# First feed-forward chunk in float32 from the arriving tiles, early loads into idle tiles of the second sweep, and early splits placed by hand

## The chip, the core and the metric

The kernel runs on one core of one Trainium2 chip. The metric is device time in microseconds (us), lower is better. The engines are TensorE (PE in the profile; its weight loads are PEld), VectorE (DVE), ScalarE (ACT), GpSimd (POOL) and SyncE (SP), which here only issues transfers. Each engine works through its own queue in the order in which it was written.

## The reference

One input x of 2048 tokens by 512 goes through two branches, mixed per token by a gate. Everything is float32.

```python
x = A_x                                              # 1 x 2048 x 512
g = sigmoid((x * gate_w).sum(-1, keepdims=True))
a = A(x)    # linear attention, 32 heads of 16
b = relu(x @ w1 + b1)**2 @ w2 + b2                   # 512 -> 1792 -> 512
out = g * a + (1 - g) * b

# A: q, k, v = x @ wqkv; pq = q @ w_phi per head, pk likewise
# phi = concat(softmax(p), softmax(-p));  kv = phi_k^T v;  z = sum of phi_k over tokens
# o = (phi_q kv) / (phi_q z + 1e-6);  A = o @ wo
```

## The kernel before

**Products in three parts.** A float32 operand is split into a high half in the format fp32r and a low half, the rest (`split`, L58: a copy on ACT, then a subtraction on DVE). A product is three matmuls that add into one PSUM bank: high by high, high by low, low by high (`mm3`, L66 to L70). A plain float32 matmul on the unsplit tiles would give the same product; the kernel uses those only for the folds (`fold`, L138: w_phi multiplied into the q or k weights), for the key-value sums (`kv_chunk`, L217) and for the numerators (`numer`, L263).

**Two sweeps.** x is worked in four blocks of 512 tokens, the hidden layer in 14 chunks of 128 columns. Sweep 0 takes, for each block, chunks 0 to 6, and beside them the k and v projections and the key-value sums; its half of the feed-forward result goes to DRAM (`part`). Sweep 1 takes chunks 7 to 13 and beside them the q projections, the division and the output projection. One step of `work_list` (L510) is one chunk of one block: an *up* product (12 matmuls of 512 columns into bank `u`), then on ACT a relu, a square and a copy, on DVE the low half (`hidden`, L301), and a *down* product (12 matmuls into four banks `d`). Up runs two steps ahead of down (`LAG`, L25). "Up 2" below is the up product of chunk 2 of the first block, and "down 0" the down product of chunk 0; "k 0", "v 0" (the first k, the first v) are projections of the first 128 tokens, also 12 matmuls each. K and v share one PSUM bank once the folds are done (L329), so each waits until the one before has been read: k by the four DVE steps in `exps` (L199 to L202), v by an ACT copy (L407).

**The order.** `at(slot, f)` (L464) hangs pieces of work on slots, two for each step, and the tile framework turns the written order and its priorities into one fixed queue for each engine; `tc.issue_after(i)` puts an instruction behind `i` on the same engine. Tiles with one tag share the buffers of that tag, so a load waits for the last reader of the buffer that it takes over. Most weights and x come through four `stage` tiles (L36, `load` L76), the fold's weights, the gate's rows of x (`gate_load` L168) and the results through six `row` tiles (L81). Tiles that only sweep 1 uses (`phiT`, `tb`, `oh`, `ol`) stand empty in sweep 0.

**The start.** `warm_up` (L350) issues 11 matmuls on zeros. `start` (L361) loads x's four parts and the first w1 chunk (a quarter and the rest on ACT's queue), splits each part as it arrives (a part of the weight on POOL, L381), and runs the first chunk's twelve products with six more zero matmuls between them (L385 to L393). W1 chunks 1 and 2 and w2 chunk 0 are split right behind (L521, L526). The other weights of sweep 0, Wv and the next block's x are each loaded and split in one step at their slots (L469 to L481), so the splits follow the arrivals.

Of the kernel before, what the change touches and what calls it, by code (L numbers as in the profile page):

```python
# [1 line left out]

# [6 lines left out]
F32 = mybir.dt.float32  # L9
# [7 lines left out]
P = 128  # L17
S, D, H, DH, F = 2048, 512, 32, 16, 1792
NK = D // P
SB = 512  # L20
# [11 lines left out]
def tile_gated_mix(ctx: ExitStack, tc: tile.TileContext, xT, xn, wqT, wkT, wphi, wv, wo, w1, b1, w2, b2, gw, out):  # L32
# [12 lines left out]
    ps_a = pool("ps_a", 1, space=PSUM)  # L45
    ps_b = pool("ps_b", 1, space=PSUM)
    banks = [ps_a, ps_b]
    taken = [0]

    def bank(name):  # L50
# [7 lines left out]
    def split(src, hi, lo, ehi, elo):  # L58
        if ehi is nc.scalar:
            i = nc.scalar.activation(hi, src, AF.Copy)  # L60
        else:
            i = ehi.tensor_copy(hi, src)
        elo.tensor_tensor(lo, src, hi.bitcast(F32), ALU.subtract)  # L63
        return i

    def mm3(o, a, b, sa, sb, first, last):  # L66
# [21 lines left out]
    def load_ffn(nm, src, fc):  # L88

        if (nm, fc) in (("w1", 1), ("w1", 2), ("w2", 0)):  # L90
            t = row()
            nc.sync.dma_start(t, src)
        else:
            t = load(src)
        hi, lo = ffn_tiles(nm, fc)
        split(t, hi, lo, nc.scalar, nc.vector)
        return hi, lo

    def load_x(b):
        xs = []  # L100
        for k in range(NK):
            t = load(xT[b, :, k, :])
            hi = xpool.tile([P, SB], F32R, tag="xh", name=f"xh{b}_{k}")
            lo = xpool.tile([P, SB], F32R, tag="xl", name=f"xl{b}_{k}")
            split(t, hi, lo, nc.scalar, nc.vector)
            xs.append((hi, lo))
        return xs

    st, up_w, down_w = {}, {}, {}
    hold = pool("hold", 2)  # L110
    ident = const.tile([P, P], F32, name="ident")
    make_identity(nc, ident)
# [25 lines left out]
    def fold(loaded, nm, k):  # L138
# [8 lines left out]
            split(ps, hi, lo, nc.scalar, nc.vector)  # L147
        return hi, lo

    def load_w(src, nm):  # L150
        res = []
        for k in range(NK):
            if nm == "o":

                t = stage.tile([P, 512], F32, tag="in", name="in")
                for q in range(4):
                    s = 64 * (4 * (k % 2) + q) + 32 * (k // 2)
                    nc.sync.dma_start(t[32 * q:32 * q + 32, :], src[s:s + 32, :])
            else:
                t = load(src[k * P:(k + 1) * P, :])  # L160
            hi = wpool.tile([P, 512], F32R, tag=f"wbh{k}", name=f"w{nm}h{k}")
            lo = wpool.tile([P, 512], F32R, tag=f"wbl{k}", name=f"w{nm}l{k}")
            split(t, hi, lo, nc.scalar, nc.vector)
            res.append((hi, lo))
        return res


    def gate_load(n):  # L168
        st["xn", n] = row()
        nc.sync.dma_start(st["xn", n], xn[n])  # L170

    def gate_chunk(n):
        t = st["xn", n]
        lg = small.tile([P, 1], F32, tag="lg", name="lg")
        nc.vector.scalar_tensor_tensor(t, t, 1.0, gwb, op0=ALU.mult, op1=ALU.mult, accum_out=lg)
        e = small.tile([P, 1], F32, tag="ge", name="ge")
        nc.scalar.activation(e, lg, AF.Exp, scale=-1.0)
        nc.vector.tensor_scalar(e, e, 1.0, None, ALU.add)
# [84 lines left out]
    def numer(pt):  # L263
# [15 lines left out]
                mm(*x)  # L279
        o = []  # L280
        for r in range(2):
            oh = work.tile([P, 512], F32R, tag=f"oh{r}", name="oh", bufs=1)
            ol = work.tile([P, 512], F32R, tag=f"ol{r}", name="ol", bufs=1)
# [31 lines left out]

    def down(t, c, dps):
        sw, b, i = work_list[t]
        mm3(dps[c], hid[t], down_w[sw * NFH + i], slice(c * P, (c + 1) * P), ALL, i == 0, i == NFH - 1)

    def do_wT(wT):  # L320
        st["wT"] = load_fold(wT)
# [9 lines left out]
    def do_w(src, nm):  # L331
        st["wb"] = load_w(src, nm)

    def do_w1_first(fc):
        with tc.issue_after(st["act0"].ins):
            do_w1(fc)

    def do_w1(fc):
        up_w[fc] = load_ffn("w1", w1[fc], fc)

    def do_w2(fc):
        down_w[fc] = load_ffn("w2", w2[fc * P:(fc + 1) * P, :], fc)

    def do_ffn(fc):
        do_w1(fc)
        do_w2(fc)

    def warm_up():  # L350
        z = st["zeros"] = work.tile([P, 512], mybir.dt.bfloat16, tag="r", name="zeros")
        nc.vector.memset(z, 0.0)
        st["warm"] = ps_a.tile([P, 512], F32, tag="s", name="warm")
        idle(11)

    def idle(n):
        for _ in range(n):
            st["up"] = nc.tensor.matmul(st["warm"], st["zeros"][:, :P], st["zeros"], start=True, stop=True)


    def start():  # L361
        t = row()
        hi, lo = up_w[0] = ffn_tiles("w1", 0)
        xs = st["x", 0] = []
        ps = ps_u.tile([P, SB], F32, tag="u", name="u")
        for k in range(NK):
            s = slice(0, P) if k == 0 else slice(P, 512)
            u = load(xT[0, :, k, :])
            if k == 0:
                for piece in (s, slice(P, 512)):  # L370
                    nc.scalar.dma_start(t[:, piece], w1[0][:, piece])
            xs.append((xpool.tile([P, SB], F32R, tag="xh", name=f"xh0_{k}"),
                       xpool.tile([P, SB], F32R, tag="xl", name=f"xl0_{k}")))
            if k == 0:
                split(t[:, s], hi[:, s], lo[:, s], nc.vector, nc.vector)
            nc.scalar.activation(xs[k][0], u, AF.Copy)
            low = nc.vector.tensor_tensor(xs[k][1], u, xs[k][0].bitcast(F32), ALU.subtract)
            if k == 0:
                rest_w = slice(P, 512)
                with tc.issue_after(low.ins):  # L380
                    split(t[:, rest_w], hi[:, rest_w], lo[:, rest_w], nc.vector, nc.gpsimd)  # L381
            (xh, xl), kk = xs[k], slice(k * P, (k + 1) * P)
            with tc.issue_after(st["up"].ins):
                st["up"] = nc.tensor.matmul(ps, hi[:, kk], xh, start=k == 0, stop=False)
            if k < 2:  # L385
                with tc.issue_after(st["up"].ins):
                    idle(2)
            with tc.issue_after(st["up"].ins):
                nc.tensor.matmul(ps, hi[:, kk], xl, start=False, stop=False)
                st["up"] = nc.tensor.matmul(ps, lo[:, kk], xh, start=False, stop=k == NK - 1)  # L390
            if k < 1:
                with tc.issue_after(st["up"].ins):
                    idle(2)  # L393
        st["u0"] = ps

    def do_x(b):
        with tc.issue_after(st["act"].ins):
            st["x", b] = load_x(b % NB)

    def do_k(b, c):  # L400
        e3, r = exps(project(c, st["x", b], st["wa"], "k"))
# [62 lines left out]
    def at(slot, f, *a):  # L464
        steps.setdefault(int(slot), []).append(lambda: f(*a))

    at(6, lambda: nc.sync.dma_start(gwb, gw.partition_broadcast(P)))
# [50 lines left out]

    warm_up()
    start()  # L520
    for fc in range(1, LAG + 1):  # L521
        do_w1(fc)
    hid[0] = hidden(0, st["u0"])
    st["act0"] = st["act"]
    with tc.issue_after(st["act0"].ins):
        for fc in range(LAG + 1):  # L526
            do_w2(fc)
    for t in range(1, LAG):
        do_up(t)
    dps = None  # L530
    for t, (sw, b, i) in enumerate(work_list):
        for f in steps.get(2 * t, ()):
            f()
        do_up(t + LAG)
        for f in steps.get(2 * t + 1, ()):
            f()
        if i == 0:
            dps = [ps_d.tile([P, 512], F32, tag="d", name=f"d{c}") for c in range(NC)]

        now = () if t == last - 1 else (t - 1, t) if t == last else (t,)  # L540
        for c in range(NC):
            for u in now:
                down(u, c, dps)
        if i < NFH - 1:
            continue
        for c in range(NC):
# [63 lines left out]
```

## Time and profile before

| | us |
|---|---|
| median of 3 runs | 533.31 (532.88 to 533.75) |
| the profiled execution, whole | 533.63 |
| its span, first to last instruction | 531.8 |

Of the 531.8 us, TensorE was busy 521.5, VectorE 355.9, ScalarE 234.7 and GpSimd 76.8. In a row of the timeline stand the start, the busy time, the engine, the line, the operation, the tiles (out<-in) with their shapes, how many instructions were merged into the row, and in brackets the idle time before it with what ended it. A float32 matmul leaves two rows. Matmuls overlap in the pipeline, and their ends are modelled: their rate is read from start to start. A row of the busy time by stage has the stage, its length, the busy time and count of each engine, the granted TensorE clock, the busy share of the DMA engines and their GB/s.

### The profile page before, as it was taken

To read this page: it belongs to the slowest core of one execution; us is meant where nothing else is said; L and a number is where in the kernel's file an instruction comes from. 1 tells how busy PE (TensorE), PEld (TensorE's weight loads), DVE (VectorE), ACT (ScalarE), POOL (GpSimd) and SP (SyncE) were. 2 spreads that over 40 slices of the span, in tenths; PEclk is the share of its full clock that TensorE was granted. 3 is DMA by queue.
4 is the path that set the end of the run, shared out by engine and by line. 5 is a ranking of instruction groups with operands and counts; after the bars stand their busy time and mean duration, and the time that the engine had idled before them with its cause. 6 is when DMAs were issued, how large, how long until landed. Compare 5 with 4: busy or idle time off the path is not lost.

```text
span 531.8 us, 8944 instructions
## 1 busy us (share of the span) xinstructions
PE 521.5 (98%) x3475; PEld 417.5 (79%) x3475; DVE 355.9 (67%) x608; ACT 234.7 (44%) x404; POOL 76.8 (14%) x60
## 2 busy tenths in 40 slices
PE   8998999999999999999999999999999999999997
PEld 3886888888888887887878878787887878787775
DVE  4688536743465434567579998998878887779423
ACT  3874333622435224254654564353435353535230
POOL 2001111111110011011103121202111111112000
PEclk9999999999999999999999999999999999999999
DMA  7974004200042000415346113134102311023102
GB/s 236 297 240 138 2 0 160 76 6 1 1 159 70 10 1 21 160 41 160 88 139 222 35 41 122 53 118 137 40 22 79 119 51 30 22 70 100 49 1 79
DMA packets 30834, 45.16 MB, mean 85 GB/s; under 512 B 5704, under 2 KB 12360, under 8 KB 30792
## 3 DMA queue, kind: packets, MB, share of 16 engines
q1 hardware_dynamic: 30328, 44.20, 27.0%
q8 instruction: 27, 0.44, 0.3%
q10 hardware_dynamic: 432, 0.39, 0.2%
q14 instruction: 15, 0.12, 0.1%
q0 software_dynamic: 32, 0.01, 0.0%
HBM read 29.89 MB, written 8.39 MB: 72 GB/s over the span
## 4 chain that ended last, share of the span: by engine, by line
PE 72%; DVE 10%; DMA 6%; SPq 5%; ACT 3%; POOL 2%; issue 2%; DVEq 0%; ACTq 0%; POOLq 0%
PE u L68 7%; PE d L69 7%; PE d L70 7%; PE d L68 7%; PE u L70 7%; PE u L69 7%; SPq L257 4%; PE v L68 3%; PE k L68 3%; PE v L69 3%; PE v L70 3%; PE k L70 3%; PE k L69 3%; PE kvps L221 2%; DMA in<-in_xT 2%; PE att L68 2%
## 5 line engine op out<-in xcount | busy, mean ns | idle before, releaser
L303 ACT ACTIVATE r<-u,b1c 128x512 f32<-128x512 f32 x56 | 38.5, 687 | 151.3 <-PE u L70 148.0
L68 PE MATMUL d<-w2h,hh 128*128 128x512 f32 x224 | 87.5, 391 | 0.0
L69 PE MATMUL d<-w2l,hh 128*128 128x512 f32 x224 | 87.3, 390 | 0.0
L70 PE MATMUL d<-w2h,hl 128*128 128x512 f32 x224 | 87.1, 389 | 0.0
L68 PE MATMUL u<-xh,w1h 128*128 128x512 f32 x220 | 86.8, 395 | 0.1
L70 PE MATMUL u<-xh,w1l 128*128 128x512 f32 x220 | 85.7, 390 | 0.5 <-DVE w1l L63 0.5
L69 PE MATMUL u<-xl,w1h 128*128 128x512 f32 x220 | 85.8, 390 | 0.0
L63 DVE TENSOR_TENSOR hl<-r,hh 128x512 fp32r<-128x512 f32 x56 | 43.0, 769 | 54.8 <-ACT hh L60 54.7
L231 POOL TENSOR_TENSOR ez<-e,z 128x512 f32<-128x512 f32 x32 | 41.4, 1317 | 188.3 <-ACT e L204 188.3
L213 POOL TENSOR_TENSOR e<-e,r 128x1024 f32<-128x1024 f32 x16 | 32.3, 2017 | 205.0 <-DVE r L209 158.3
L207 DVE TENSOR_REDUCE sm<-e 128x64 f32<-128x1024 f32 x32 | 39.0, 1218 | 28.5 <-ACT e L204 28.4
L68 PEld LDWEIGHTS u<-xh,w1h 128*128 128x128 f32 x220 | 41.3, 188 | 12.0 <-issue 1.6
L70 PEld LDWEIGHTS d<-w2h,hl 128*128 128x128 f32 x224 | 42.0, 188 | 8.7
L68 PEld LDWEIGHTS d<-w2h,hh 128*128 128x128 f32 x224 | 42.0, 188 | 8.7
L69 PEld LDWEIGHTS d<-w2l,hh 128*128 128x128 f32 x224 | 42.1, 188 | 8.6
L70 PEld LDWEIGHTS u<-xh,w1l 128*128 128x128 f32 x220 | 41.3, 188 | 9.5 <-DVE w1l L63 0.9
L69 PEld LDWEIGHTS u<-xl,w1h 128*128 128x128 f32 x220 | 41.3, 188 | 8.2
L204 ACT ACTIVATE e<-e 128x1024 f32<-128x1024 f32 x32 | 33.8, 1055 | 23.7 <-DVE e L202 23.5
L255 ACT ACTIVATE phiT<-tb 32x256 f32<-32x256 f32 x64 | 26.5, 413 | 35.1 <-DVE tb L249 34.4
L60 ACT ACTIVATE hh<-r 128x512 fp32r<-128x512 f32 x56 | 35.2, 628 | 1.3
L304 ACT ACTIVATE r<-r 128x512 f32<-128x512 f32 x56 | 35.1, 627 | 1.0
L199 DVE TENSOR_REDUCE mx<-k 128x32 f32<-128x512 f32 x16 | 11.0, 688 | 26.3 <-PE k L70 26.3
(106 smaller groups left out, 888.5 us busy)
## 6 DMA issues: line engine op xcount, KB each, us to landing
in<-in_xT SPq DMA_DIRECT2D x32, 256.0 KB, 3.9
in<-in_w SPq DMA_DIRECT2D x24, 256.0 KB, 3.2
phiT<-tb SPq DMA_DIRECT2D x192, 32.0 KB, 1.8
row<-in_xn SPq DMA_DIRECT2D x16, 256.0 KB, 3.2
part<-row SPq DMA_DIRECT2D x16, 256.0 KB, 2.0
row<-part SPq DMA_DIRECT2D x16, 256.0 KB, 3.5
out<-row SPq DMA_DIRECT2D x15, 256.0 KB, 2.2
row<-in_wkT SPq DMA_DIRECT2D x4, 256.0 KB, 6.0
```

The costliest lines, as they stand in the source:

```text
L60: i = nc.scalar.activation(hi, src, AF.Copy)
L63: elo.tensor_tensor(lo, src, hi.bitcast(F32), ALU.subtract)
L68: nc.tensor.matmul(o, ah[:, sa], bh[:, sb], start=first, stop=False)
L69: nc.tensor.matmul(o, ah[:, sa], bl[:, sb], start=False, stop=False)
L70: return nc.tensor.matmul(o, al[:, sa], bh[:, sb], start=False, stop=last)
L204: nc.scalar.activation(ef, ef, AF.Exp)
L207: nc.vector.tensor_reduce(sm, e3, AX.X, ALU.add)
L213: eng.tensor_tensor(e3, e3, w.unsqueeze(2).to_broadcast([P, 2 * H, DH]), ALU.mult)
L231: nc.gpsimd.tensor_tensor(ez[:, hs, :], e3[:, hs, :], zbc[half], ALU.mult)
L255: nc.scalar.activation(dst, src, AF.Copy)
L303: nc.scalar.activation(r, ps, AF.Relu, bias=b1c[:, fc:fc + 1])
L304: nc.scalar.activation(r, r, AF.Square)
```

## The change

- The first chunk of the first block is four plain float32 matmuls on the tiles as they arrive. The low and high halves of x are still made, for the chunks after it; those of the first w1 chunk are made later, as the second block needs them. There are 8 zero matmuls ahead and none between.
- Loading (`fetch`) and splitting (`ready`) are separate. The first loads are issued one after the other at the start: x into a `phiT` tile, w1 chunks 0 to 2 and w2 chunk 0 into `tb` tiles, then w1 3, w2 1, the fold's weights, w1 4, w2 2, then Wv into the `phiT` tile again. Later blocks' x goes through `tb` tiles, the gate's rows through `oh` and `ol` tiles (now two of each tag in place of one each of four).
- Splits are hung on slots of their own and, with `issue_after`, behind the copy of the newest hidden tile on ACT (`st["act"]`) and the gate's product behind the newest subtraction on DVE (`st["low"]`).
- Up 1 follows the float32 chunk, down follows up and up follows down, by `issue_after`, in the first steps.

The queue of PE after the change has the same order as before from down 0 on, but for a few neighbours swapped. On DVE and ACT the order between down 0 and the end of sweep 0 is another: the halves of later weights, of Wv and of the next x, and the gate's products, stand further behind.

```diff
+    def ready_later(nm, fc):
+        with tc.issue_after(st["act"].ins):
+            ready(nm, fc)
...
     def gate_load(n):
-        st["xn", n] = row()
-        nc.sync.dma_start(st["xn", n], xn[n])
+        t = st["xn", n] = work.tile([P, D], F32, tag="ol" if n % 2 else "oh", name="xn", bufs=2)
+        nc.sync.dma_start(t, xn[n])
...
+        with tc.issue_after(st["low"].ins):
+            nc.vector.scalar_tensor_tensor(t, t, 1.0, gwb, op0=ALU.mult, op1=ALU.mult, accum_out=lg)
...
     def start():
-        t = row()
-        hi, lo = up_w[0] = ffn_tiles("w1", 0)
...
+        t = work.tile([P, 2, 4, NG, 32], F32, tag="phiT", name="xin", bufs=1).rearrange("p u r g s -> p (u r g s)")
+        w = [work.tile([P, 2 * D], F32, tag="tb", name="win", bufs=2) for _ in range(2)]
+        raw["w1", 0] = w[0][:, :D]
+        xs = [t[:, k * D:(k + 1) * D] for k in range(NK)]
+        for k in range(NK):
+            nc.sync.dma_start(xs[k], xT[0, :, k, :])
+        for s in (slice(0, P), slice(P, 512)):
+            nc.scalar.dma_start(w[0][:, s], w1[0][:, s])
+        fetch("w1", 1, w[0][:, D:])
+        fetch("w1", 2, w[1][:, :D])
+        fetch("w2", 0, w[1][:, D:])
+        fetch("w1", 3)
+        fetch("w2", 1)
+        st["wT"] = load_fold(wkT)
+        fetch("w1", 4)
+        fetch("w2", 2)
...
+            with tc.issue_after(st["up"].ins):
+                st["up"] = nc.tensor.matmul(ps, raw["w1", 0][:, kk], xs[k], start=k == 0, stop=k == NK - 1)
+            hi, lo = x_tiles(0, k)
+            split(xs[k], hi, lo, nc.scalar, nc.vector)
+            st["x", 0].append((hi, lo))
+        ready("w1", 1)
+        hid[0] = hidden(0, ps)
+        ready_later("w1", 2)
+        ready_later("w2", 0)
+        with tc.issue_after(st["up"].ins):
+            do_up(1)
+        ready_later("w1", 0)
+        fetch_v()
...
     for fc in range(LAG + 1, NFH):
-        at(2 * (fc - LAG) - 2, do_w1_first, fc)
-        at(2 * (fc - LAG) - (2 if fc == LAG + 1 else 1), do_w2, fc)
-    at(0, do_wT, wkT)
+        at(2 * (fc - LAG) - (2 if fc == LAG + 1 else 1), ready_later, "w1", fc)
+    for fc in range(1, NFH):
+        at(2 * fc - 1, ready_later, "w2", fc)
+    for nm, fc, s in (("w1", 5, 2), ("w2", 3, 2), ("w1", 6, 4), ("w2", 4, 4), ("w2", 5, 6), ("w2", 6, 8)):
+        at(s, fetch, nm, fc)
...
-    at(1, do_w, wv, "v")
+    for k in range(NK):
+        at(5 + k // 2, v_ready, k)
     for b in range(NB):
         for c in range(NC):
-            s = b * SL + 3 * c - 3 if b else 7 + c
+            s = b * SL + 3 * c - 3 if b else 3
             at(s, gate_load, b * NC + c)
-            at(s + 3, gate_chunk, b * NC + c)
-        at(b * SL + 4, do_x, b + 1)
+            at(s + 3 if b else 8 + c, gate_chunk, b * NC + c)
+        at(b * SL + 4, x_fetch, b + 1)
+        for k in range(NK):
+            at(b * SL + 7 + k // 2, x_ready, b + 1, k)
...
-        do_up(t + LAG)
+        with tc.issue_after(st["down"].ins) if 0 < t <= LAG else nullcontext():
+            do_up(t + LAG)
...
+        with tc.issue_after(st["up"].ins) if t < LAG else nullcontext():
+            for c in range(NC):
+                for u in now:
+                    down(u, c, dps)
```

More of the change, by code (lines that the diff above doesn't have):

```diff
@@ L1 @@
[L1 removed]
+from contextlib import ExitStack, nullcontext
 import concourse.bass as bass
@@ L107, in load_x, with x_fetch, x_ready @@
         return xs
-    st, up_w, down_w = {}, {}, {}
+    def x_fetch(b):
+        for k in range(NK):
+            if k % 2 == 0:
+                t = work.tile([P, 2 * D], F32, tag="tb", name="xin", bufs=2)
+            raw["x", b, k] = t[:, (k % 2) * D:(k % 2 + 1) * D]
+            nc.sync.dma_start(raw["x", b, k], xT[b % NB, :, k, :])
+    def x_ready(b, k):
+        hi, lo = x_tiles(b, k)
+        with tc.issue_after(st["act"].ins):
+            split(raw.pop(("x", b, k)), hi, lo, nc.scalar, nc.vector)
+        st.setdefault(("x", b), []).append((hi, lo))
     hold = pool("hold", 2)
@@ L353, in warm_up @@
         st["warm"] = ps_a.tile([P, 512], F32, tag="s", name="warm")
[L354 to L358, printed above, removed]
+        for _ in range(8):
+            st["up"] = nc.tensor.matmul(st["warm"], z[:, :P], z, start=True, stop=True)
     def start():
-        t = row()
-        hi, lo = up_w[0] = ffn_tiles("w1", 0)
-        xs = st["x", 0] = []
+        t = work.tile([P, 2, 4, NG, 32], F32, tag="phiT", name="xin", bufs=1).rearrange("p u r g s -> p (u r g s)")
@@ L365, in start @@
+        fetch("w2", 1)
+        st["wT"] = load_fold(wkT)
+        fetch("w1", 4)
+        fetch("w2", 2)
         ps = ps_u.tile([P, SB], F32, tag="u", name="u")
+        st["x", 0] = []
         for k in range(NK):
[L367 to L373, printed above, removed]
@@ L520, in tile_gated_mix @@
     start()
[L521 to L529, printed above, removed]
     dps = None
```

91 lines of the change are left out of this document (41 added, 50 removed).

## The prediction

> **What bounds the kernel now.** I read the head of the page, then the busy time by stage, then TensorE's own timeline wherever a stage shows idle time, then the queues of ScalarE (ACT) and VectorE (DVE) around those places.
>
> ```profile
> span 531.8 us, 8944 instructions
> PE 521.5 (98%) x3475; PEld 417.5 (79%) x3475; DVE 355.9 (67%) x608; ACT 234.7 (44%) x404; POOL 76.8 (14%) x60
> ```
> ```profile
> core 0: us, PE busy (x) PEld busy (x) DVE busy (x) ACT busy (x) POOL busy (x), PEclk, DMA share, GB/s
> 0.00:17.50 17.50, 15.18 (x54) 8.78 (x55) 7.77 (x14) 9.12 (x15) 2.82 (x11) 1.00 0.81 252
> 17.50:47.00 29.50, 27.33 (x134) 22.13 (x132) 25.32 (x57) 23.33 (x46) 1.61 (x1) 1.00 0.72 221
> 47.00:250.00 203.00, 203.00 (x1737) 165.15 (x1738) 108.17 (x192) 77.45 (x127) 28.81 (x16) 1.00 0.19 61
> 250.00:500.00 250.00, 248.65 (x1412) 200.12 (x1411) 206.09 (x335) 119.48 (x210) 43.61 (x33) 1.00 0.28 82
> ```
>
> TensorE (PE) is the bound: without a gap from 47 to 250 us, 1.35 us idle in the next 250. What it does there is the same after the change, in the same order but for a few swaps of neighbours, so a microsecond gained before 47 us should reach the end. All that can be had is ahead of 47 us. The first stage looks busy (15.18 of 17.5), but much of that is warm-up:
>
> ```profile
> 1.19 4.87 PE L358 MATMUL warm<-zeros 128*128 128x512 bf16 x11 [1.19 <-DVE zeros L352]
> ...
> 8.98 0.49 PE L389 MATMUL u<-xl,w1h 128*128 128x512 f32 x1 [0.55 <-DVE xl L377]
> ...
> 10.79 0.50 PE L70 MATMUL u<-xh,w1l 128*128 128x512 f32 x1 [0.46 <-DVE w1l L63]
> ...
> 12.96 0.39 PE L390 MATMUL u<-xh,w1l 128*128 128x512 f32 x1
> ...
> 17.50 0.39 PE L68 MATMUL d<-w2h,hh 128*128 128x512 f32 x1
> ...
> 22.94 1.95 PE L142 MATMUL foldk<-row 128*128 128x128 f32 x16
> 24.64 0.48 PE L68 MATMUL d<-w2h,hh 128*128 128x512 f32 x1
> ...
> 27.23 0.39 PE L70 MATMUL d<-w2h,hl 128*128 128x512 f32 x1
> 27.74 2.35 PE L142 MATMUL foldk<-row 128*128 128x128 f32 x16
> 29.85 0.47 PE L68 MATMUL u<-xh,w1h 128*128 128x512 f32 x1
> ...
> 40.63 0.39 PE L70 MATMUL u<-xh,w1l 128*128 128x512 f32 x1
> 41.82 0.47 PE L68 MATMUL v<-wvh,xh 128*128 128x512 f32 x1 [0.81 <-DVE e L202]
> ...
> 45.35 0.39 PE L68 MATMUL d<-w2h,hh 128*128 128x512 f32 x1
> 46.94 0.50 PE L68 MATMUL k<-wkh,xh 128*128 128x512 f32 x1 [1.21 <-ACT vext L407]
> 47.28 0.40 PE L69 MATMUL k<-wkl,xh 128*128 128x512 f32 x1
> ```
>
> Starts give the true rate: 20 matmuls of 512 columns from 12.96 to 17.50 are **0.227 us** each; twelve (one up chunk, one down chunk, one projection) are 2.72. So the 36 matmuls ahead of the first down chunk at 17.50 are 8.2 us of work. Later losses: the second pair of folds is due at 27.46 and over at 29.85, 2.39 us where the first pair took 1.70: **0.69**. The first v projection is due at 40.86 and starts at 41.82: **0.96**. The second k is due at 45.58 and starts at 46.94: **1.36**. After a wait the first matmul takes 0.34 (46.94 to 47.28), 0.11 over.
>
> **The change, part by part.** *The float32 chunk.* Removed: twelve split products, nine of 17 warm-up matmuls, and the weight's subtraction on GpSimd (POOL); its split for later blocks moves behind up 1. Added: four float32 matmuls straight from the arrived tiles. The folds are float32: eight matmuls of 128 columns, 16 rows, in 1.70 us (22.94 to 24.64), 0.21 each, so 0.85 for 512 columns; four passes at 0.227 would be 0.91. I take 0.9, 3.6 for the chunk, 0.9 more than twelve products. If the passes ran at the warm-up's pace (11 matmuls in the 4.31 us from 1.19 to the first real one at 5.50, about 0.43 each) it would be 1.7 each, the high end. What it waits for are arrivals:
>
> ```profile
> 4.55 0.63 ACT L376 ACTIVATE xh<-in 128x512 fp32r<-128x512 f32 x1 [1.60 <-DMA in<-in_xT]
> ...
> 7.58 1.27 ACT L376 ACTIVATE xh<-in 128x512 fp32r<-128x512 f32 x2 [0.22 <-DMA in<-in_xT]
> 8.91 1.29 ACT L60 ACTIVATE w1h<-row 128x512 fp32r<-128x512 f32 x2
> 13.39 0.69 ACT L303 ACTIVATE r<-u,b1c 128x512 f32<-128x512 f32 x1 [3.19 <-PE u L390]
> 14.11 0.63 ACT L304 ACTIVATE r<-r 128x512 f32<-128x512 f32 x1
> 14.78 0.63 ACT L60 ACTIVATE hh<-r 128x512 fp32r<-128x512 f32 x1
> 15.31 0.62 ACT L60 ACTIVATE w2h<-row 128x512 fp32r<-128x512 f32 x1
> ```
> ```profile
> 6.93 0.36 DVE L62 CAST w1h<-row 128x384 fp32r<-128x384 f32 x1 [1.03 <-DMA row<-in_w]
> 7.40 2.73 DVE L377 TENSOR_TENSOR xl<-in,xh 128x512 fp32r<-128x512 f32 x3
> ...
> 16.65 1.29 DVE L63 TENSOR_TENSOR w2l<-in,w2h 128x512 fp32r<-128x512 f32 x2
> ```
>
> The loads ahead of this point keep their order, so x's parts arrive as before (4.5, 6.7, 7.5, by 8.2) and the rest of the weight at 6.93. Float32 matmul one runs at 4.75; two at 6.95, with 0.11 restart to 7.96; three to 8.86; four to **9.76**. The idle time between one and two costs nothing: nothing else has arrived.
>
> *What is late next.* ACT's spacing, from the rows above: relu 0.43 after the last matmul's start (12.96, 13.39), square 0.72 on, copy 0.67 on, an independent copy 0.53 on. DVE: 0.60 per subtraction, 0.68 until done. Next chunk (up 1): its high half is done at 9.54 as before; DVE subtracts x's fourth part from 8.87 and this weight from 9.56, done 10.25; its third matmul, due 10.21, waits 0.04; the chunk ends at about 12.6. For up 2 ACT now runs relu 9.97, square 10.69, copy 11.36, weight copy 11.89 to 12.51; DVE takes the hidden tile's low half first (12.02) and the weight's at 12.62, done 13.30. Up 2's third matmul, due 13.05, waits 0.25; it ends at 15.67. Down 0 starts there (its weight's low half done by 13.9), not at 17.50: **1.83 gained**.
>
> *Places of the splits.* Down 0 and up 3 go to 21.1, folds to 22.8, down 1 to 25.55. The second folds need both banks back: the last subtraction of the first pair comes after relu 21.3, square 22.0, fold copy 22.55, hidden copy 23.1, fold copy 23.6, so DVE is done at 25.05: 0.5 to spare, **0.69 gained**. Up 4 at 27.25 needs a split done at 25.65. First v, due 38.15, needs the k bank read:
>
> ```profile
> 39.20 0.69 DVE L199 TENSOR_REDUCE mx<-k 128x32 f32<-128x512 f32 x1
> ...
> 41.00 0.68 DVE L202 TENSOR_TENSOR e<-mn,k 128x512 f32<-128x512 f32 x1
> ...
> 45.64 2.23 DVE L63 TENSOR_TENSOR hl<-r,hh 128x512 fp32r<-128x512 f32 x1
> ```
> ```profile
> 45.39 1.93 POOL L213 TENSOR_TENSOR e<-e,r 128x1024 f32<-128x1024 f32 x1 [37.01 <-DVE ge L178]
> ```
> ```profile
> 46.31 0.58 ACT L407 ACTIVATE vext<-v 128x512 f32<-128x512 f32 x1
> ```
>
> Before, k 0 ended at 35.4 and DVE turned to it at 39.20, behind gate products, splits and the next block's x. These stand later in the new queue: only the hidden tile's and one weight's subtraction precede (done 33.5), k 0 ends at 32.7, so the four steps run 33.4 to 35.9, 2.2 us ahead of need: **0.96 and the 0.11 gained**. Wv's last part is subtracted by 40.4, needed at 40.65. Second k, due 42.2, waits for v's copy: ACT has relu, square and four copies ahead from 38.35, so the copy runs 41.85 to 42.42; 0.25 and a restart stay of 1.36 and a restart, **1.1 gained**. Second v, due 49.4, is about where DVE finishes the second k, because POOL's product (1.93) holds up a subtraction beside it (2.23 for 0.68): **0.1 lost**.
>
> *Transfers.* At the first stage's 252 GB/s a 256 KB tile takes 1.04 us. The fold's weights are 15th, nine behind the one landed by 8.91, so by 18.3, needed 21.1; weight tile five is the 23rd, by 27, needed 32. SP's queue then waits for staging tiles that the subtractions above free (the next by 19.2, 25.65, 33.5); x's next block, queued between, is first copied at 41.3. So the loads lie under the matmuls; uncovered, one late tile costs its own 1 us. The gate rows and x parts in tiles of the second sweep cost nothing: from 47 to 250 PE never waited, ACT was busy 77 and DVE 108 of 203 us. After 250 the moved splits may take away or add a part of the 1.35 us idle there, 0.7 either way, and I take 0.
>
> Sum: 1.83 + 0.69 + 1.07 + 1.1 - 0.1 = **4.6 us**. The profiled execution took 533.6 us in all, 1.8 over its span, and becomes 529.0; the median of the runs shown is 533.31 and becomes **528.7**.
>
> **Weighing a rule.** Granted clock reads 1.00 in every stage, yet warm-up matmuls start 0.43 apart and real ones 0.227, so PE begins at half pace and steps up at about 5.5. The Trainium skill ("TensorE: Matmul & The Clock Gate", part 1, on the HAM clock gate) says that the array starts at half clock, is released after about one busy window of 3.4 us whose phase is free, and falls back after an idle one. It speaks against the cut to eight warm-ups: they cover just that window. No row here shows the phase moving.
>
> **Rivals.**
> *A, only the start is won.* The splits from 20 to 47 us are as late as before relative to PE, since ACT and DVE are as loaded (23.33 and 25.32 of 29.5 us) and margins of 0.04 to 0.5 us are all there is. Then 533.31 - 1.83 = 531.5; half of the later gains, 530.1. Against it: the k bank has 2.2 us to spare.
> *B, the full pace comes later.* It came 4.3 us after the first matmul (1.19 to 5.50). Eight warm-ups end at 4.6 and the second float32 matmul waits till 6.95; if the count starts again there, the pace is half until 11.25, 2.15 us are lost, and the time is 530.9. For it: less early work. Against: as in C. By the window of the Trainium skill's page named above, the step would come one window after 5.5, at about 8.9, an estimate, which would lose 1.0 and give 529.7.
> *C, slower: half pace lasts through up 2.* From 6.95 every microsecond at half pace costs half of it; 4.6 is gone when it lasts past 16.2, and at 20 the loss is 6.5, so 535.2. For it: less work early, and a gap of 0.9 us or more before 6.95. Against: in the trace the pace holds over 0.55, 0.46 and 1.21 us of idleness (47.28 follows 46.94 by 0.34).
> *D, more:* stalls after 250 us vanish as well, 527.4 to 528.
> *E, nothing:* float32 matmuls take 1.7 each and A holds too. The chunk ends at 12.2 instead of 9.76, 2.4 later, of which the waits of 0.04 and 0.25 behind it take up 0.3: 533.31 - 1.83 + 2.4 - 0.3 = 533.6.
>
> **Numbers.** Forecast 0.57, A 0.19, B 0.09, D 0.07, C 0.05, E 0.03. The forecast's own range is 527.9 to 529.6. Range 527.2 to 531.2: down to D, up through B and most of A, leaving out C, E and A's worst end, about 0.15. About 0.2% is what this kernel's runs can tell from no change: faster 0.92, within 0.02, slower 0.06.
>
> **What would show it.** Four float32 matmuls (eight rows) ending near 9.8; first down chunk near 15.7; second folds without a gap; first v within 0.1 of its due time; second k 0.2 to 0.4 late; then all earlier by 4 to 5 us to the end. It is wrong if spacing after 7 us is 0.43, if a matmul waits over 0.5 us for a weight's subtraction or a landing before 47 us, or if gaps over 0.5 us appear between 47 and 250.

## The result, and the profile after

| | us |
|---|---|
| median after, 6 runs | 529.42 (529.11 to 529.91) |
| median before beside it, 6 runs | 533.96 (532.88 to 535.33) |
| ratio, 95% interval | 0.9921 (0.9907 to 0.9935) |
| the profiled execution after, whole | 529.36 |

The kernel became 0.8% faster, by 4.5 us between the medians and by 4.27 us between the profiled executions. The head of the page after:

```profile
span 527.6 us, 8895 instructions
PE 520.0 (99%) x3462; PEld 415.7 (79%) x3462; DVE 362.8 (69%) x606; ACT 236.3 (45%) x405; POOL 77.0 (15%) x59
```

The busy time by stage after:

```profile
0.00:17.50 17.50, 16.05 (x50) 8.81 (x51) 7.45 (x12) 12.18 (x19) 1.82 (x10) 1.00 0.90 312
17.50:47.00 29.50, 29.42 (x146) 24.57 (x145) 20.65 (x33) 17.57 (x32) 2.19 (x1) 1.00 0.48 166
47.00:250.00 203.00, 202.94 (x1739) 164.60 (x1738) 119.67 (x211) 82.74 (x136) 29.35 (x15) 1.00 0.21 67
250.00:500.00 250.00, 248.49 (x1406) 199.19 (x1404) 207.91 (x341) 118.84 (x212) 43.65 (x33) 1.00 0.27 81
```

From 17.5 to 47 us TensorE now has 0.08 us without work where it had 2.17. VectorE is busy 20.65 us there instead of 25.32, ScalarE 17.57 instead of 23.33: their work has moved behind 47 us (VectorE 119.67 instead of 108.17), where it held TensorE up once, by some 0.3 us (the third k, below). The first stage moves 312 GB/s instead of 252. TensorE's timeline after, at the places that the prediction names:

```profile
4.76 1.65 PE L415 MATMUL u<-xin,win 128*128 128x512 f32 x2
6.67 2.84 PE L415 MATMUL u<-xin,win 128*128 128x512 f32 x6 [0.26 <-DMA win<-in_w]
9.32 0.50 PE L69 MATMUL u<-xh,w1h 128*128 128x512 f32 x1
...
15.38 0.39 PE L69 MATMUL d<-w2h,hh 128*128 128x512 f32 x1
...
25.35 1.95 PE L170 MATMUL foldk<-row 128*128 128x128 f32 x16
27.05 0.48 PE L69 MATMUL u<-xh,w1h 128*128 128x512 f32 x1
...
38.03 0.39 PE L69 MATMUL v<-wvh,xh 128*128 128x512 f32 x1
...
42.35 0.50 PE L69 MATMUL k<-wkh,xh 128*128 128x512 f32 x1
...
46.58 0.39 PE L69 MATMUL u<-xh,w1h 128*128 128x512 f32 x1
...
49.51 0.47 PE L69 MATMUL v<-wvh,xh 128*128 128x512 f32 x1
```

The first down chunk starts at 15.38 instead of 17.50, the second folds take 1.70 us instead of 2.39, the first v waits for nothing, and k and v behind it wait about 0.2 each.

How far ahead of before TensorE is, start by start: 2.11 us at the first down chunk, 2.80 at up 4 behind the folds, 5.03 at the up behind the second k, 4.82 at the second v, 4.57 at the third k (70.57 instead of 75.14), 4.39 at 250 us, 4.86 at the first q, 4.46 after the first numerators, 4.24 after the last ones. Two rows of before, the up behind the second k and the first of q's folds:

```profile
51.61 0.39 PE L68 MATMUL u<-xh,w1h 128*128 128x512 f32 x1
```
```profile
252.75 1.13 PE L142 MATMUL foldq<-row 128*128 128x128 f32 x8 [0.57 <-PE d L68]
```

So 5.03 us were won by 47 us, and 4.24 are left. In between, 0.8 us came on top at the first of q's folds, where the wait of 0.57 is gone, and 0.2 by the first q; lost were 0.6 up to 250 us, 0.5 at the third of q's folds, 0.4 at the first numerators and 0.2 at the last. The first numerators, after, then before:

```profile
309.69 1.09 PE L312 MATMUL num<-phiT,kvb 64*32 64x256 f32 x30 [0.84 <-DMA phiT<-tb]
```
```profile
314.15 1.09 PE L268 MATMUL num<-phiT,kvb 64*32 64x256 f32 x30 [0.45 <-DMA phiT<-tb]
```

The same wait for the turned q tiles is 0.4 us longer, since TensorE came earlier than q's chain of VectorE steps and transfers did.

### The profile page after: what moved, and what is told of

Read it like the earlier page. It is cut to its first block, busy times and chain, and to the rows that moved or that the text cites. A ratio compares the mean times of both kernels' runs of the same rounds, so it can differ in the third digit from the quotient of the medians.

```text
span 527.6 us, 8895 instructions
## 1 busy us (share of the span) xinstructions
PE 520.0 (99%) x3462; PEld 415.7 (79%) x3462; DVE 362.8 (69%) x606; ACT 236.3 (45%) x405; POOL 77.0 (15%) x59
## 4 chain that ended last, share of the span: by engine, by line
PE 76%; DVE 10%; SPq 4%; ACT 3%; DMA 2%; POOL 2%; issue 2%; DVEq 0%; ACTq 0%; POOLq 0%
PE u L69 8%; PE u L71 7%; PE u L70 7%; PE d L69 7%; PE d L70 7%; PE d L71 7%; SPq L301 4%; PE k L69 3%; PE v L69 3%; PE k L70 3%; PE k L71 3%; PE v L70 2%; PE v L71 2%; POOL ez L275 2%; PE att L69 2%; PE att L70 2%
## 5 line engine op out<-in xcount | busy, mean ns | idle before, releaser
L257 POOL TENSOR_TENSOR e<-e,r 128x1024 f32<-128x1024 f32 x16 | 33.4, 2087 | 209.7 <-DVE r L253 145.7
L591 DVE SCALAR_TENSOR_TENSOR row<-d,rest,row 128x512 f32<-128x512 f32 (+1 forms) x33 | 22.4, 729 | 6.3 <-PE d L71 6.1
```

Of the source, the lines that this page charges most:

```text
L257: eng.tensor_tensor(e3, e3, w.unsqueeze(2).to_broadcast([P, 2 * H, DH]), ALU.mult)
```

## The experiments

Theory: the start is won by the float32 chunk, the rest by places on the queues and by transfers that leave early; each needs its part of the change. The main rival: one part does nearly all. Each series has its own runs of the kernel before on the same chip; ratios are against those. Ratios have intervals of about 0.14% each way, so two runs of different series are told apart from some 1 us on.

| run | what it is | median, us | before, us | ratio (95%) |
|---|---|---|---|---|
| e1_split_first | after, first chunk split again | 530.51 | 533.61 | 0.9941 (0.9927 to 0.9954) |
| e2_f32_alone | before, with float32 chunk | 536.0 | 533.61 | 1.0042 (1.0029 to 1.0056) |
| e3_no_places | after, no places by hand | 529.31 | 533.61 | 0.9917 (0.9904 to 0.993) |
| e4_old_buffers | after, gate rows and x in old buffers | 533.63 | 533.61 | 1.0 (0.9989 to 1.001) |
| e13_gate_rows | after, gate rows in old buffers | 529.53 | 533.12 | 0.9934 (0.9922 to 0.9945) |
| e11_v_staged | after, Wv through staging | 529.53 | 534.21 | 0.9902 (0.9882 to 0.9921) |
| e12_bias_on_pool | before, four bias rows on GpSimd | 533.52 | 534.21 | 0.9984 (0.9973 to 0.9994) |
| e5_one_warm | after, 1 warm-up | 530.69 | 533.58 | 0.9952 (0.9939 to 0.9964) |
| e6_twelve_warm | after, 12 warm-ups | 529.37 | 533.58 | 0.9926 (0.9914 to 0.9939) |
| e7_late_num | after, first and last numerators later | 527.76 | 533.58 | 0.9895 (0.988 to 0.9911) |
| e8_late_num_x | e7, and x's splits later | 528.21 | 533.58 | 0.991 (0.9895 to 0.9926) |
| e9_last_num_x | after, last numerators and first x splits later | 527.57 | 534.21 | 0.9872 (0.9854 to 0.989) |

### The float32 chunk undone

```diff
-                st["up"] = nc.tensor.matmul(ps, raw["w1", 0][:, kk], xs[k], start=k == 0, stop=k == NK - 1)
+                st["up"] = mm3(ps, up_w[0], st["x", 0][k], kk, ALL, k == 0, k == NK - 1)
```
(and the two VectorE splits of the weight ahead of it)

> The changed kernel with one part undone: the first chunk is multiplied as twelve split products again, its weights split on VectorE in two pieces as they come; loads, buffers and places stay. My theory (float32 on TensorE frees ACT and VectorE ahead of up 1, and early loads and places do the rest): up 1's low part of the weights comes 0.6 to 1.0 us later, the first down chunk starts at about 16.3 instead of 15.38, and nothing later takes it back: 0.8 to 1.0 us over the changed kernel, about 530.3. Rival 1, the float32 product is the whole gain at the start: 2.1 us over it, about 531.5. Rival 2, the product's precision does not matter because the transfers bound the start either way: within 0.2 us of it.

The medians lie 1.1 us apart, about as much as two series can tell, the profiled executions 0.5 (528.1 and 527.6 of span), and the sign is that of the theory. Its path is not. The low part of up 1's weights was done as early as in the changed kernel (9.24 and 9.30 on VectorE); the time went into the chunk itself, which starts at 5.28 instead of 4.76 because it waits for ACT's high half of x, and then waits for x's low parts:

```profile
5.28 0.55 PE L69 MATMUL u<-xh,w1h 128*128 128x512 f32 x1 [0.50 <-ACT xh L61]
6.01 0.50 PE L70 MATMUL u<-xl,w1h 128*128 128x512 f32 x1 [0.17 <-DVE xl L64]
```

The first down chunk starts at 15.92. With the arrivals of x it moves between runs that keep the changed kernel's float32 start, eight warm-ups included: e8_late_num_x has it at 15.31, with x's second part copied by ACT at 6.05, and e7_late_num at 16.07, with the copy at 7.17. This run copies it at 6.17 and is 0.6 us behind the one with like arrivals. So inside the changed kernel the float32 product is worth 0.6 us by the traces and 1.1 by the medians.

### The float32 chunk alone

```diff
-                st["up"] = nc.tensor.matmul(ps, hi[:, kk], xh, start=k == 0, stop=False)
+                st["up"] = nc.tensor.matmul(ps, t[:, kk], u, start=k == 0, stop=k == NK - 1)
...
-        idle(11)
+        idle(8)
...
+        split(st["t0"], *up_w[0], nc.scalar, nc.vector)
```
(and up 1 behind the chunk by `issue_after`)

> The kernel before with one part of the change done: eight warm-up products, then the first chunk as four float32 products as the pieces of x arrive, its weights split for later blocks behind the first activations; all loads and places as before. My theory (the gains do not add up: the same loads and the same ACT queue still set when the second folds, the first v and the second k can run): the first down chunk starts about 2 us earlier, but the second folds, v and k then wait the longer, and 0.2 to 1.2 us are left of it: about 532.8 to 533.8 beside 534.0 for the kernel before. Rival, each part is worth its own start gain: 2.1 us, about 531.9.

Worse than either theory: 0.4% over the kernel before. The start was won in full, for the first down chunk began at 14.93, 2.6 us earlier than before, and at the first v TensorE was 3.6 us ahead. At the second k it was 1.1 ahead, at the up behind it 0.3 behind, at the end 0.6 behind. TensorE, then ACT and VectorE of this run:

```profile
41.91 0.39 PE L69 MATMUL d<-w2l,hh 128*128 128x512 f32 x1
45.84 0.50 PE L68 MATMUL k<-wkh,xh 128*128 128x512 f32 x1 [3.54 <-ACT vext L392]
...
47.17 0.63 PE L70 MATMUL k<-wkh,xl 128*128 128x512 f32 x1
...
50.16 0.52 PE L70 MATMUL d<-w2h,hl 128*128 128x512 f32 x1
```
```profile
42.67 0.19 ACT L177 ACTIVATE ge<-lg 128x1 f32<-128x1 f32 x1
44.58 0.72 ACT L538 ACTIVATE row<-b2b,rest 128x512 f32<-128x512 f32 x1 [1.72 <-DVE rest L181]
45.21 0.58 ACT L392 ACTIVATE vext<-v 128x512 f32<-128x512 f32 x1
```
```profile
42.14 2.33 DVE L175 SCALAR_TENSOR_TENSOR row<-row,gwb 128x512 f32<-128x512 f32 x1
...
44.40 0.14 DVE L181 TENSOR_SCALAR rest<-gate 128x1 f32<-128x1 f32 x1
```

ACT's queue holds v's copy behind a row that needs the gate (`rest`), and the small VectorE step that writes `rest` stands behind a gate product that takes 2.33 us, beside a product of GpSimd that runs from 41.62 to 43.93. The k bank is free only when v has been copied. Work resumes at full pace at 45.84, after 3.5 us without; 1.3 us later the products fall to half pace, from 47.17 to 50.16, which the granted clock of that stretch shows:

```profile
47.20:50.20 3.00, 3.00 (x9) 2.35 (x8) 0.47 (x2) 0.20 (x1) 0.00 (x0) 0.50 0.35 87
50.20:52.00 1.80, 1.80 (x9) 1.51 (x8) 1.59 (x3) 0.00 (x0) 0.00 (x0) 0.94 0.00 0
```

Seven products there took 2.99 us instead of 1.59, 1.4 us more. So it is the half pace that turns a gain of 1.1 at the second k into a loss. This execution was also the fastest of nine (534.23; the median is 536.0). Over the whole execution its granted clock is 0.996, that of the execution at the median 0.993: 0.003 of 534 us is 1.6 us, by estimate most of the 1.8 between them. Where those others lost it no trace shows.

### The places undone

```diff
 def ready_later(nm, fc):
-        with tc.issue_after(st["act"].ins):
-            ready(nm, fc)
+        ready(nm, fc)
```
(and likewise in `x_ready`, `v_ready` and `gate_chunk`)

> The changed kernel without the places set by hand: the early splits of weights, x, v's weights and the gate's sums are free to go where the scheduler puts them; float32 product, loads and buffers stay. My theory: splits that are not yet due sit in the ACT and VectorE queues ahead of the folds' low parts and k's reductions, so that the waits at the second folds, v and k come back: 1.5 to 2.5 us over the changed kernel, about 531 to 532. Rival, the early transfers alone do it and the queues have slack enough: 0 to 0.3 us over it.

The rival was right on the time: the median is that of the changed kernel. The folds and the first v ran without a gap as there. One wait did come back:

```profile
PE k L69 <- ACT vext L435: 1.1, 1, 1.1
```

TensorE was 1.42 us behind the changed kernel at the up behind it, 0.5 of it from a start whose x arrived later (its second part is copied at 7.12 instead of 6.46). It made up 0.2 at the second v, 0.4 by the third k and its down chunk, 0.4 at q's folds, since the changed kernel waits there and this one, coming later, does not; 0.4 is left at the end. The places by hand buy the second k and nothing else, and most of that is given back.

### The early buffers undone, in three steps

```diff
-                t = work.tile([P, 2 * D], F32, tag="tb", name="xin", bufs=2)
-            raw["x", b, k] = t[:, (k % 2) * D:(k % 2 + 1) * D]
-            nc.sync.dma_start(raw["x", b, k], xT[b % NB, :, k, :])
+            raw["x", b, k] = load(xT[b % NB, :, k, :])
...
-        t = st["xn", n] = work.tile([P, D], F32, tag="ol" if n % 2 else "oh", name="xn", bufs=2)
+        t = st["xn", n] = row()
```

> The changed kernel with its early transfers partly undone: the gate's rows of x and the next block of x go through the staging buffers of the kernel before again and wait for those; the first x and weights, v's weights, the float32 product and the places stay. My theory (the early buffers for v and for the first weights carry the gain, these two are covered by other work): 0 to 0.5 us over the changed kernel. Rival, every transfer must leave early since the staging buffers hold up the loads queued behind them: 1 us or more over it, with waits on TensorE at second k and v.

The whole gain is gone, but not where the rival put it. Up to 47 us TensorE runs as in the changed kernel, 0.4 us later from the first down chunk on; the second v waits 0.87 us, and the rest stands where the second sweep begins. TensorE's waits of this run from 245 to 320 us, and what SP's queue waited for:

```profile
PE num L309 <- DMA phiT<-tb: 2.5, 2, 1.3
PE foldq L167 <- DVE wql L64: 1.3, 1, 1.3
PE kvt L468 <- DVE row L457: 0.8, 1, 0.8
```
```profile
SPq L79 <- DVE xl L64: 15.0, 4, 14.4
```
```profile
258.34 0.63 ACT L61 ACTIVATE w1h<-in 128x512 fp32r<-128x512 f32 x1 [1.73 <-DMA in<-in_w]
...
259.50 0.58 ACT L61 ACTIVATE wqh<-foldq 128x512 fp32r<-128x512 f32 x1
```

Four pieces of x, loaded ahead of their splits, sit in the four staging tiles. The second sweep's weights wait on SP for 14.4 us, come late, and ACT, which takes things in order, holds the folded q weights behind them. That is the cost of a load that is issued early into a buffer which others need, and not what x's early transfer is worth against the kernel before, which loaded and split x in one step. Which of the two edits it was, the next run tells; it keeps x early and puts only the gate's rows back:

> The changed kernel with one of the two early transfers undone that the run with the old staging buffers undid together: the gate's rows of x go back into the small row buffers, while the next block of x keeps its early place outside the staging buffers. That run lost 4.2 us, nearly all of it after 250 us, in waits on TensorE that ended with weights coming late through the staging buffers. My theory (the loss is x's alone: four pieces of x held the four staging buffers until their splits, and the second sweep's weights queued behind them): 0 to 0.5 us over the changed kernel, no wait over 0.7 us between 250 and 300 us. Rival (the gate's rows hold the row buffers that the folds' weights need, so that they count too): 1 to 4 us over it, with a longer wait at the folds near 258 us.

Within what can be told of the changed kernel, and no wait of TensorE came up that it doesn't have too. So the gate's rows alone lose nothing; it takes x's pieces in the staging tiles (x's pieces alone were not run).

The third early transfer is Wv's:

```diff
-        fetch_v()
...
-        at(5 + k // 2, v_ready, k)
+    at(1, do_w, wv, "v")
```

> The changed kernel with one early transfer undone: v's weights go through the four staging buffers at their place of before and are split as they come, and no longer early into the second sweep's transfer buffer; float32 product, gate rows, x blocks and the other places stay. My theory (the early buffer is what lets v's weights pass while the staging buffers wait for splits): weights queue behind them, the first v waits 0.5 to 1.5 us again, or up 4 and down 3 do: 0.8 to 2.5 us over the changed kernel. Rival, v's weights would be there in time through the staging buffers too, since the float32 product and the other buffers have emptied the queue: within 0.3 us of it.

The rival was right: 529.53 beside 529.42. Up 4 waited 0.3 us for a subtraction at 27.8, the first v did not wait, and the second v's 0.2 was gone.

### The gate's chain in the kernel before

```diff
-                nc.scalar.activation(o, b2b, AF.Copy, scale=rest[:, n:n + 1])
+                if b == 0:
+                    nc.gpsimd.tensor_scalar(o, b2b, rest[:, n:n + 1], None, ALU.mult)
+                else:
+                    nc.scalar.activation(o, b2b, AF.Copy, scale=rest[:, n:n + 1])
```

> The kernel before with one edit: in the first block the four rows of bias times one minus gate are made on GpSimd instead of ACT, so that ACT's copy of the first v no longer stands behind four rows that wait for the gate. My theory (the second k's wait of 1.37 us in the kernel before is the gate's chain: ACT's queue holds v's copy behind a row that waits for the gate of x's rows, whose transfers come late; moving the gate's rows ahead is what removed that wait): the second k waits 0 to 0.4 us and the time is 0.6 to 1.4 us under the kernel before. Rival: the copy, or the bank, is held by something else (VectorE's steps for the first k), and the wait stays, or GpSimd's rows slow VectorE beside them: within 0.3 us of the kernel before, or over it.

0.7 us faster by the medians, which is the theory's time; but the wait is 1.0 instead of 1.2, which is the rival's. The profiled execution, the longest of the twelve, has no gain (TensorE 0.07 us earlier at the up behind the second k, 0.4 later at the end), so no trace shows where the 0.7 was won. The rows are gone from ACT's queue, but the gate's exponent is not:

```profile
45.62 0.20 ACT L177 ACTIVATE ge<-lg 128x1 f32<-128x1 f32 x1 [1.44 <-DVE row L175]
...
46.24 0.58 ACT L407 ACTIVATE vext<-v 128x512 f32<-128x512 f32 x1
```

It stands ahead of v's copy and waits for the gate's product on VectorE. So v's copy still stands behind the gate's chain, and this edit took only one of its links out. The same run shows how an early gain is absorbed. In it TensorE was 0.68 us earlier at the second folds, and the first v waited the longer:

```profile
41.99 0.47 PE L68 MATMUL v<-wvh,xh 128*128 128x512 f32 x1 [1.65 <-DVE e L202]
```

It starts at 41.99 where it started at 41.82: in both runs VectorE's queue sets that time, and not what TensorE does ahead of it.

### The warm-up

```diff
-        for _ in range(8):
+        for _ in range(1):
```
(and `range(12)` in the other run)

> The changed kernel with one warm-up product instead of eight, so that TensorE stands idle from about 1.6 us until the first piece of x is there at 4.76. In the changed kernel's rows the products run at half pace (0.43 us for 512 columns, then 1.01 and 0.90 for the halves of the first float32 product) until some 5.5 to 6.5 us, about 4.3 to 5 us after the first warm-up. My theory (the pace rises only after 4 us or more of work on end, idle time does not count): half pace lasts until about 9 us, the four float32 products end about 1.2 us later, at 10.5, and the time is 0.8 to 1.4 us over the changed kernel. Rival (the pace rises a fixed time after the start, with or without work): within 0.2 us of it.

> The changed kernel with twelve warm-up products instead of eight. My theory: they end at about 6.1 to 6.3 us, all at half pace but the last; the float32 products then run at full pace, 0.86 us each, and end at 9.6 to 9.8 where they ended at 9.32: 0.2 to 0.5 us over the changed kernel. Rival: the last pieces of x bind the end of the first chunk, so that a later start of it costs nothing: within 0.1 us.

With one product, the first chunk ran at half pace up to its last product:

```profile
1.19 0.61 PE L390 MATMUL warm<-zeros 128*128 128x512 bf16 x1 [1.19 <-DVE zeros L387]
4.74 6.27 PE L415 MATMUL u<-xin,win 128*128 128x512 f32 x8 [2.94 <-DMA win<-in_w]
10.44 0.79 PE L69 MATMUL u<-xh,w1h 128*128 128x512 f32 x1
```

The eight halves take 6.27 us where the changed kernel's rows have 1.65 and 2.84, the chunk ends 1.1 us later, and the median is 1.3 us over the changed kernel: the theory, the pace rises by work and not by time. With twelve the median is the same, which is the rival's time. (The profiled execution was 0.6 us longer, with its first down chunk at 15.98, which lies within what e7_late_num and e8_late_num_x show for eight.) By the medians, eight to twelve is flat.

```profile
1.19 5.30 PE L390 MATMUL warm<-zeros 128*128 128x512 bf16 x12 [1.19 <-DVE zeros L387]
6.29 3.85 PE L415 MATMUL u<-xin,win 128*128 128x512 f32 x8
```

### Taking back what was given back

```diff
+        put = p == 0 or late
-        at(s + 12 - 2 * late, finish, n, n % NC)
-        at(s + 13 - 2 * late, finish, n + 1, n % NC + 1)
+        at(s + 12 - 2 * late + put, finish, n, n % NC)
+        at(s + 13 - 2 * late + put, finish, n + 1, n % NC + 1)
...
-        at(s + 10 - 2 * late, do_n, p)
+        at(s + 10 - 2 * late + put, do_n, p)
```

> The changed kernel with the first and the last pair's numerators and their outputs one step of the order later, since TensorE waits there for the turned q transfers (1.11 us at 308.5 and 1.12 us at 499.4 in the changed kernel, 0.71 and 0.87 before). My theory (these waits are slack that the earlier start of all else cannot use, since q's chain of VectorE steps and transfers sets the time of the numerators; a step later other products stand there): both waits go, 1.5 to 2.2 us under the changed kernel, about 527.2 to 527.9. Rival: the wait moves to the output products behind the numerators, or to the end, where the last output is late: 0 to 0.5 us under it.

The time is the theory's, 1.7 us under the changed kernel by the medians; the way there is half the theory's and half the rival's. The last pair's wait is gone for good, and with it 1.5 us: TensorE is 0.49 behind the changed kernel ahead of that pair, and 1.00 ahead of it at the end. The first pair's came back at the next q and brought 0.1:

```profile
316.65 0.50 PE L69 MATMUL q<-wqh,xh 128*128 128x512 f32 x1 [1.09 <-DVE ol L64]
```

Q's bank is one that the numerators' splits still read. The second run also hung x's splits one slot later, `at(b * SL + 8 + k // 2, ...)`:

> The same as the run before it, and the splits of the next block of x one step of the order later, so that the second chunk's k and v no longer find them ahead of the copy of v and of k's reductions (waits of 0.24 and 0.21 us at 42.1 and 49.3 in the changed kernel). My theory: 0.2 to 0.6 us under the run before it. Rival: x's splits then come too late for the next block's first product, or collide with others, and nothing or up to 1 us is lost.

The rival: the second v's wait went, and 0.73 us came up at 196.3, where an up product's second matmul, which reads x's low part, now waited for VectorE, whose subtraction took 2.41 us there. The last version takes only the two edits that cost nothing elsewhere: the last pair one slot later (`- late` for `- 2 * late`), and `7 + (b == 0) + k // 2` for x's splits.

> The changed kernel with only the last pair's numerators and outputs one step later, and only the first block's splits of the next x one step later. In the run that moved both pairs, the first pair's wait came back as 1.25 us at the next q, whose bank the numerators' splits still read; in the run that moved all of x's splits, a wait of 0.73 us came up at the third block's end. My theory: the last pair's 1.1 us and the second v's 0.2 us are gone and nothing new comes: 527.4 to 528.2, 1.2 to 2.0 us under the changed kernel. Rival: the last pair's step only looked free beside the first pair's, or x's splits cost as much elsewhere: 0 to 0.6 us under it.

527.57, the lowest median of all: 1.3% under the kernel before and 1.9 us under the changed kernel by the medians, 1.5 of it at the last pair. TensorE's waits from 20 us to its end are down to these three:

```profile
PE num L312 <- DMA phiT<-tb: 0.9, 1, 0.9
PE foldq L170 <- DVE wql L64: 0.2, 1, 0.2
PE att L69 <- DVE ol L64: 0.2, 1, 0.2
```

## Why the prediction was right

528.7 was forecast and 529.42 measured; the range held it. The gain was forecast at 4.6 us, and is 4.54 between the medians and 4.27 between the profiled executions; the median of the kernel before is 533.96 over six runs where the forecast started from 533.31. Point by point, gains by the distance between the two TensorE timelines:

| step | forecast, us | measured, us |
|---|---|---|
| first down chunk | 1.83 | 2.11 |
| second folds | 0.69 | 0.69 |
| first v, second k, with restarts | 2.17 | 2.23 |
| second v | -0.1 | -0.21 |
| from there to 250 us | 0 | -0.4 |
| after 250 us | 0 (0.7 either way) | -0.1 |

- *The start.* The float32 chunk ends at 9.32, not 9.76. Its second product starts at 6.67, not 6.95, as what it waits for was there sooner; the full-pace halves start 0.43 us apart, so a product is 0.86 where 0.9 was taken. The first product ran at half pace, as the forecast feared for one product and not for all. That the sum comes so close is in part luck. The start's 0.28 beyond the forecast is that of the arrivals (x's second part is copied at 6.46, before at 6.74), and it covers half of the later losses. Arrivals move the start from run to run: between 15.31 and 16.07 for the first down chunk in the runs that keep this start, and at 17.03 instead of 17.50 in e12_bias_on_pool, whose start is that of before.
- *Folds, first v, second k.* All as worked out, the wait of 0.24 at the second k included: ACT's copy of v runs from 41.72, forecast 41.85.

```profile
41.72 0.58 ACT L439 ACTIVATE vext<-v 128x512 f32<-128x512 f32 x1
```

- *Mis-sized: the cover from 47 to 250 us.* The prediction had no loss there; 0.4 us was lost. The third k waits, and what holds it up is again the gate's chain:

```profile
66.03 2.42 DVE L219 SCALAR_TENSOR_TENSOR xn<-xn,gwb 128x512 f32<-128x512 f32 x1
```
```profile
68.49 0.20 ACT L221 ACTIVATE ge<-lg 128x1 f32<-128x1 f32 x1 [3.60 <-DVE xn L219]
69.31 0.73 ACT L582 ACTIVATE row<-b2b,rest 128x512 f32<-128x512 f32 x1 [0.61 <-DVE rest L225]
69.94 0.58 ACT L439 ACTIVATE vext<-v 128x512 f32<-128x512 f32 x1
```

A gate product of 2.42 us, beside a product of GpSimd from 65.74 to 67.90, holds the exponent, the row and then v's copy. An average of 77 busy us of 203 on ACT said nothing about one queue at one place.

- *Rivals.* A, only the start: no, 2.9 us came behind it. B and C, the pace: no in this kernel, since all is at full pace by 7.2 us. That rival's mechanism is real, though: e2_f32_alone fell back to half pace, 1.3 us behind an idle time of 3.5 us, and lost 1.4 us. The Trainium skill ("TensorE: Matmul & The Clock Gate", part 1) says that the array falls back after an idle window of about 3.4 us; here 3.5 us did it, with that delay, and 1.2 us (the kernel before, at 46.94) did not. D, stalls after 250 us vanish: no. The numerators' waits grew from 1.1 to 1.7 us in all, those at q's folds fell from 0.6 to 0.2.
- *What the forecast did not ask.* It gave each part of the change its own gain. The runs show that the parts don't add: the float32 chunk is worth 2.6 us of start alone and ends up as a loss, and 0.6 to 1.1 us inside the changed kernel; the places by hand, the gate's buffers and Wv's buffer can each be undone at no cost that shows. What none of these runs undid by itself is the separation of loading and splitting, with its order of loads and its later slots. It is what is left to carry the folds and the first v, but that is argued, not shown.

## What to carry to other kernels

An engine's start is worth only what the next queue lets through: before pricing a gain, find the next instruction whose time is set by another engine's order (here VectorE's steps for the first k, and the gate's chain in front of ACT's copy of v) and price both together. Where a VectorE instruction will run beside one of GpSimd's, price it to the end of GpSimd's (up to 2.4 us here, and not 0.7). A load that is issued long ahead of its use wants a buffer that nobody else is queued for. When a kernel gets faster at the front, look at the waits that grow behind, and move the waiting work by a slot; that was another 1.9 us here.

## What the runs showed of the hardware beyond that

Behind three of the waits above (e2_f32_alone's second k, the changed kernel's third k, e8_late_num_x's up product) stands a VectorE instruction that ran beside GpSimd's product of k's exponentials. One pair, GpSimd's and VectorE's:

```profile
39.95 2.19 POOL L257 TENSOR_TENSOR e<-e,r 128x1024 f32<-128x1024 f32 x1 [37.18 <-DVE r L253]
```
```profile
40.28 2.41 DVE L64 TENSOR_TENSOR hl<-r,hh 128x512 fp32r<-128x512 f32 x1
```

From 15 to 250 us of the changed kernel, eleven of VectorE's 122 products and subtractions start while such a product of GpSimd runs. Wherever in it they start, all end 0.55 to 0.6 us behind GpSimd's end, and so take from 0.69 to 2.43 us. VectorE's small steps on one number per row (0.15 us each) that start in these stretches are not longer there. So in these traces the long steps are held until GpSimd is done, and not slowed. In the prediction this is the subtraction of 2.23 us; where the next one would fall was not asked.

The granted clock reads 1.00 from the start while products of 512 columns start 0.43 us apart; in the stretch from 47.2 to 50.2 us of e2_f32_alone it reads 0.50 at the same spacing. So the column shows a later fall and not the first slow stretch, and the pace is read from start to start. The step to full pace moves between runs: in e6_twelve_warm products are still 0.43 apart at 6.29, 5.1 us after the first, while in e7_late_num the first float32 product is at full pace at 5.17, 4.0 us after the first: its two halves take 1.12 us where they take 1.65 in the changed kernel:

```profile
5.17 1.12 PE L415 MATMUL u<-xin,win 128*128 128x512 f32 x2 [0.38 <-DMA win<-in_w]
```

The same section of the Trainium skill calls the window free-running and lets the step vary by about 0.5 us either way; here it moved by over 1 us.
